# Seven products for eight in every pair's second matrix, and blocks 0 and 1 led through the first matrix together

## The chip, the core and the metric

One core of a Trainium2 chip runs the whole program. The metric is device time of one execution in microseconds (us). The engines of the core are TensorE (PE in the rows: matrix products), VectorE (DVE), ScalarE (ACT), GpSimd (POOL, all but unused here) and SyncE (SP, which issues every transfer). PEld is TensorE's loading of weights, which overlaps the products.

## What is computed

```python
# q, k, v: (8, 8, 576, 64)
k_s = softmax(k, axis=2);  q_s = softmax(q, axis=-1)
kv  = einsum('bhsd,bhse->bhde', k_s, v)
x   = einsum('bhsd,bhde->bhse', q_s, kv)          # 4608 rows of 512
h   = x @ w_in                                    # 512 x 2048
x2  = relu(h)**2 @ w_out                          # 2048 x 512
y   = sigmoid(x2 @ w_gate) * (x2 @ w_val)         # 512 x 1536 each
out = y @ w_out2                                  # 1536 x 512
```

The weights arrive as 64-bit floats, so each 128x512 tile of them is first rebuilt as a 32-bit float by ScalarE and VectorE.

## The kernel before

**Tiles.** The 4608 rows are nine blocks of 512. Every 32-bit factor is split into a high part (a copy to the matrix type, by ScalarE) and a low part (the difference, by VectorE, line 214). `mm3` (lines 217 to 219) makes one product from three matmuls: high·high, high·low, low·high. One matmul has 128x128 weights against 128x512 columns.

**Stages.** Blocks 0, 1 and 2 go through both matrices with plain products while the weights are still being rebuilt: `c_in` multiplies by the first matrix into banks 4 and 5, `c_g` (ScalarE) squares the relu out of the bank into a tile `g0`, `c_hi` and `c_lo` split it, `c_out` multiplies by the second matrix into banks 0 to 3. For each block that is 16 slices f of 12 matmuls in and 12 out. Blocks 3 to 8 go in three pairs (`in_stage`), and then all nine blocks go in five gate stages (`gate_stage`: sigmoid, product, last matrix).

**Seven products.** Where two blocks are taken together, a two-by-two block product is made of seven products of sums instead of eight products (`PRODUCTS`, `plan_seven`). The sums of weights are made once (`plan_sums`). The sums of the data (`plan_b`, `b_comb`, line 671) are VectorE's, and so are the additions of each product out of its bank (`e_add`, line 733). All first matrices of pairs and gates are made so, and the last matrices. The second matrix of a pair is made so only if the pair's number is in `OUT7`, which holds 2, the last pair; pairs 0 and 1 use eight products (`o_mm`).

**Order.** A planner (`Plan`) writes the order of each engine's instructions before the program runs. Each step has a due time (T0, T2, T3 and so on with a step per slice), an engine with a cost, the steps that it waits for, and the buffers that it takes and gives back (`SIZES`: 14 of X, 11 of W, 6 of S, 19 of f, 8 of x). The planner takes the earliest due step that is ready, so a step without urgency fills a gap. Each engine then runs its own list strictly in order, and SyncE its list of transfers.

**Beside the stages** run the k and q steps of later blocks (softmax, small matmuls at lines 440, 452, 467, 524, 577; `plan_blocks`), and the rebuilding, summing, splitting and storing of the gate weights (`plan_w`, spread from T4 until the first gate stage). Split weights are stored to DRAM and fetched again as tiles `ws` for each use. Block 0 uses the tiles `whl` as they are made; block 1 fetches all 16 pieces of the first matrix again. The stages' order is pair 0, pair 1, gate 0, gate 1, pair 2, gates 2 to 4, and the k and q steps for pair 2 stand beside gate 1.

Of the kernel before, what the change touches and what calls it, by code (L numbers as in the profile page):

```python
# [15 lines left out]
AF = mybir.ActivationFunctionType  # L16
# [126 lines left out]
def attention_mlp_mlp(  # L143
# [20 lines left out]
    nc = tc.nc  # L164
    NB, NP, _, N = q.shape
# [5 lines left out]
    KT = DM // 128  # L171
    F1 = w_out.shape[0]
    F2 = w_out2.shape[0]
    wide = w_in.dtype == I64

    OUT7 = (2,)
    SIZES = {"X": 14, "W": 11, "S": 6, "f": 19, "x": 8, "q": 3, "a": 6, "w": 5, "k": 2, "v": 2, "km": 1, "kr": 2, "pa": 2, "qm": 4, "qr": 4}
    cst = ctx.enter_context(tc.tile_pool(name="cst", bufs=1))
    p4 = ctx.enter_context(tc.tile_pool(name="p4", bufs=1))
# [19 lines left out]
    LOW = {DVE: TT}  # L199
# [25 lines left out]
    wf = {}  # L225
# [172 lines left out]

    fetched, xorder, sorder = [], [], []

    def plan_fetch(key, use, t):

        add(t, {DMA: 1.5}, ("wf", use), w_fetch, key, use, after=[("ws",) + key], take=["W"])
        fetched.append(("wf", use))


# [84 lines left out]
    NONE = 3  # L491
# [104 lines left out]
    x_before = {}  # L596
# [105 lines left out]
    freed = {x: [] for x in pairs}  # L702
# [95 lines left out]
    g0 = {}  # L798
    x2d = {}
    z_t = {}  # L800

    def c_use(j, kind, g, i):

        return ("c%d" % j, kind, g, i) if j else (kind, g, i)

    def c_in(j, f, kt):

        g, r = divmod(f // 2, 2)
        w = whl[c_use(j, "in", g, (1, 2, 0, 4)[2 * r + kt // 2])]
        c = 256 * (kt % 2) + 128 * (f % 2)  # L810
        x = x_t[j, kt]
        mm3(banks[4 + f % 2], w[:, 0, c:c + 128], w[:, 1, c:c + 128], x[:, 0], x[:, 1], kt == 0, kt == KT - 1)

    def c_g(j, f):
        t = tile2("f", "g0")
        nc.scalar.activation(out=t, in_=banks[4 + f % 2], func=AF.Relu)
        nc.scalar.activation(out=t, in_=t, func=AF.Square)
        g0[j, f] = t

# [94 lines left out]
    MM = 0.227  # L914
    MH = 0.1185
    NU = F1 // 4
    T0, TS0, TS1 = 30.0, 4.45, 6.2
    TS2 = 3.4
    T2 = T0 + TS0 * F1
    T3 = T2 + TS1 * F1  # L920
    T4 = T3 + TS1 * F1
    T1 = T4 + TS2 * F1 + 4
# [12 lines left out]

    def conv_fetch(j, kind, g, ii, t):

        if j:
            for i in ii:
                plan_fetch((kind, g, i), c_use(j, kind, g, i), t - 14)  # L940

    def conv_in(j, f, t):

        ready = lambda i: ("wf", ("c%d" % j, "in", g, i)) if j else ("wo", "in", g, i)
        tag = "W" if j else "X"
        g, r = divmod(f // 2, 2)
        if f % 2 == 0:
            conv_fetch(j, "in", g, ((1, 2), (0, 4))[r], t)
        for kt in range(KT):
            i = (1, 2, 0, 4)[2 * r + kt // 2]  # L950
            if kt:
                wait = [("ch", j, f, kt - 1)]
            elif f > 1:
                wait = [("cg", j, f - 2)]
            else:
                wait = [("cg", j - 1, F1 - 2 + f)] if j else []
            add(
                t, {PE: 3 * MM}, ("ch", j, f, kt), c_in, j, f, kt,
                after=[("x", j, kt), ready(i)] + wait, give=[XTAG[j]] if f == F1 - 1 else [],
            )  # L960
            if f % 2 and kt % 2:
                add(t, {FREE: 0.0}, ("cf", j, f, kt), lambda: None, after=[("ch", j, f, kt)] + ([] if j else [("ws", "in", g, i)]), give=[tag])
        add(t + 2.6, {ACT: 1.17}, ("cg", j, f), c_g, j, f, after=[("ch", j, f, KT - 1)], take=["f"])

    def conv_out(j, f, t):

        ready = lambda i: ("wf", ("c%d" % j, "out", g, i)) if j else ("wo", "out", g, i)
        tag = "W" if j else "X"
        g, r = divmod(f // 2, 2)
        ii = ((1, 0), (2, 4))[r]  # L970
        if f % 2 == 0:
            conv_fetch(j, "out", g, ii, t)
        add(t - 2.5, {ACT: AS}, ("chi", j, f), c_hi, j, f, after=[("cg", j, f)], take=["S"])
        add(t - 2, LOW, ("clo", j, f), c_lo, j, f, CHOSEN, after=[("chi", j, f)], give=["f"])
# [23 lines left out]
    freed[4, 5] = (T4, [("cg", j, F1 - 2), ("cg", j, F1 - 1)])  # L998

    done_b = {0}  # L1000

    def plan_blocks(js, t, per):

        for j in js:
            new = [b for _, b in segs(j) if b not in done_b]
            done_b.update(new)
            for p in range(NP):
                for b in new:
                    plan_k(b, p, t, 1.0, x_before.get(j, []))
                plan_q(j, p, t + 2, 1.0)  # L1010
                t += per / NP
# [50 lines left out]
    IN = [tuple(range(j, j + 2)) for j in range(NONE, NB, 2)]  # L1062
# [221 lines left out]
    plan_blocks([1], T0 + 6, TS0 * F1 - 20)  # L1284
    plan_blocks([2], T2 + 6, TS1 * F1 - 30)
    plan_blocks(IN[0], T3 + 5, (T1 - T3 - 40) / 2)

    BESIDE = {0: 1, 3: 2}
    t = T1
    for i, (stage, n) in enumerate(STAGES):  # L1290
        if i in BESIDE:
# [6 lines left out]
        t = stage(n, t)  # L1298
# [71 lines left out]
```

## Time and profile before

| | |
|---|---|
| median of 3 runs | 1684.14 us (1682.77 to 1688.67) |
| the profiled execution's own time | 1689.22 us |
| its span, first to last instruction | 1687.4 us |
| mean granted TensorE clock | 0.992 of full |

The page gives an engine's busy time and its count of instructions over the span. Its slices of 42 us show where the load lies. Busy TensorE time is modelled and overlaps from one matmul to the next, so rates are read from the distance between starts.

### The profile page before, as it was taken

Reading aid. Unit: us, or ns where it says so; the run is one execution under the profiler, and the core shown is the slowest. Engines: PE = TensorE matmul, PEld = TensorE weight load, DVE = VectorE, ACT = ScalarE, POOL = GpSimd, SP = SyncE. Lnnn points to the kernel's source line nnn. Section 1 sums busy time; section 2 is a strip of 40 time slices with the busy share of each in tenths; the row PEclk is TensorE's granted clock in tenths of the full one; section 3 lists DMA queues with packets and bytes.
Section 4 is the critical chain, followed back from the end, with each engine's and each line's share of the span. In section 5 each row is a group of like instructions: output and inputs, shape, how many; then the busy total and the mean of one; then the engine's idle time right before and its main releaser. Section 6 shows DMA issues by size and latency. Waiting matters only on the chain.

```text
span 1687.4 us, 24273 instructions
## 1 busy us (share of the span) xinstructions
PE 1651.6 (98%) x8740; PEld 1416.2 (84%) x8740; DVE 1158.9 (69%) x2178; ACT 927.6 (55%) x1632; POOL 1.9 (0%) x14
## 2 busy tenths in 40 slices
PE   6899999999999999999999999999999999999999
PEld 4677788878888888888898889988888899889998
DVE  8988846788889656865774758665954583448446
ACT  5876645567477657643454556464733453335344
POOL 0000000000000000000000000000000000000000
PEclk9998999999999999999999999999999999999999
DMA  7998899798897979899567555867786667555796
GB/s 287 343 359 327 305 360 334 278 342 343 298 347 256 369 256 351 303 335 355 188 191 243 191 186 164 274 201 250 243 291 195 191 210 240 191 196 185 246 377 253
DMA packets 153175, 457.90 MB, mean 271 GB/s; under 512 B 16096, under 2 KB 25312, under 8 KB 153056
## 3 DMA queue, kind: packets, MB, share of 16 engines
q1 hardware_dynamic: 153056, 456.36, 77.4%
q8 instruction: 69, 1.13, 0.3%
q14 instruction: 50, 0.41, 0.1%
HBM read 360.35 MB, written 95.94 MB: 270 GB/s over the span
## 4 chain that ended last, share of the span: by engine, by line
PE 90%; DVE 5%; DMA 2%; ACT 2%; issue 1%; SPq 0%; ACTq 0%; DVEq 0%
PE bank L217 29%; PE bank L219 28%; PE bank L218 28%; PE kps L467 2%; PE xps L577 2%; DMA ws<-w_in 1%; DVE bX L214 0%; DMA wraw<-in_moe_w_out_dram 0%; DVE whl L214 0%; DVE bS L214 0%; DMA kt<-in_k_dram 0%; DVE xf L671 0%; PE qsw L524 0%; DVE wf L277 0%; DVE s L671 0%
## 5 line engine op out<-in xcount | busy, mean ns | idle before, releaser
L217 PE MATMUL bank<-bX,ws 128*128 128x512 f32 (+1 forms) x1176 | 447.2, 380 | 3.2 <-DMA ws<-w_in 3.2
L218 PE MATMUL bank<-bX,ws 128*128 128x512 f32 (+1 forms) x1176 | 441.3, 375 | 0.0
L219 PE MATMUL bank<-bX,ws 128*128 128x512 f32 (+1 forms) x1176 | 441.2, 375 | 0.0
L733 DVE TENSOR_TENSOR s<-s,bank 128x512 f32<-128x512 f32 (+1 forms) x285 | 184.4, 652 | 206.6 <-PE bank L219 170.6
L211 ACT ACTIVATE s<-bank 128x512 f32<-128x512 f32 (+1 forms) x285 | 161.4, 570 | 225.9 <-PE bank L219 223.5
L217 PEld LDWEIGHTS bank<-bX,ws 128*128 128x128 f32 x1176 | 222.4, 189 | 42.3 <-ACT bS L211 3.5
L219 PEld LDWEIGHTS bank<-bX,ws 128*128 128x128 f32 x1176 | 222.1, 189 | 40.4
L218 PEld LDWEIGHTS bank<-bX,ws 128*128 128x128 f32 x1176 | 222.5, 189 | 37.9 <-issue 0.7
L211 ACT ACTIVATE bS<-s 128x512 fp32r<-128x512 f32 (+1 forms) x298 | 174.9, 598 | 124.4 <-PE bank L219 113.0
L214 DVE TENSOR_TENSOR bS<-s,bS 128x512 fp32r<-128x512 f32 (+1 forms) x298 | 191.6, 652 | 57.5 <-ACT bS L211 57.0
L217 PE MATMUL bank<-ws,bS 128*128 128x256 f32 x756 | 214.7, 284 | 0.0
L219 PE MATMUL bank<-ws,bS 128*128 128x256 f32 x756 | 214.1, 283 | 0.4 <-DVE bS L214 0.4
L218 PE MATMUL bank<-ws,bS 128*128 128x256 f32 x756 | 214.0, 283 | 0.0
L752 ACT ACTIVATE s<-s 128x512 f32<-128x512 f32 (+1 forms) x120 | 70.5, 589 | 140.2 <-DVE s L733 139.9
L217 PEld LDWEIGHTS bank<-ws,bS 128*128 128x128 f32 x756 | 145.0, 192 | 1.4 <-ACT s L211 0.3
L218 PEld LDWEIGHTS bank<-ws,bS 128*128 128x128 f32 x756 | 145.0, 192 | 1.0 <-issue 0.2
L219 PEld LDWEIGHTS bank<-ws,bS 128*128 128x128 f32 x756 | 145.0, 192 | 0.6 <-DVE bS L214 0.6
L217 PE MATMUL bank<-bS,ws 128*128 128x512 f32 x368 | 144.6, 393 | 0.2 <-issue 0.2
L218 PE MATMUL bank<-bS,ws 128*128 128x512 f32 x368 | 143.3, 389 | 0.0
L219 PE MATMUL bank<-bS,ws 128*128 128x512 f32 x368 | 143.3, 389 | 0.0
L211 ACT ACTIVATE whl<-wf 128x512 fp32r<-128x512 f32 x127 | 78.3, 626 | 50.1 <-DVE wf L284 27.8
L214 DVE TENSOR_TENSOR whl<-wf,whl 128x512 fp32r<-128x512 f32 x127 | 85.9, 689 | 10.1 <-ACT whl L211 9.9
(118 smaller groups left out, 2425.3 us busy)
## 6 DMA issues: line engine op xcount, KB each, us to landing
ws<-w_gv SPq DMA_DIRECT2D x210, 512.0 KB, 4.4
ws<-w_out SPq DMA_DIRECT2D x197, 512.0 KB, 4.3
ws<-w_in SPq DMA_DIRECT2D x116, 512.0 KB, 6.1
w_out<-whl SPq DMA_DIRECT2D x53, 512.0 KB, 4.7
w_gv<-whl SPq DMA_DIRECT2D x42, 512.0 KB, 6.2
w_in<-whl SPq DMA_DIRECT2D x32, 512.0 KB, 4.9
wraw<-in_moe_w_out_dram SPq DMA_DIRECT2D x28, 512.0 KB, 6.6
vt<-in_v_dram SPq DMA_DIRECT2D x32, 325.0 KB, 6.5
```

The source lines that it names most:

```text
L211: nc.scalar.activation(out=dst, in_=src, func=AF.Copy)
L214: by_name[engine].tensor_tensor(out=dst, in0=src, in1=hi.bitcast(F32), op=ALU.subtract)
L217: nc.tensor.matmul(ps, ah, bh, start=first, stop=False, skip_group_check=True)
L218: nc.tensor.matmul(ps, ah, bl, start=False, stop=False, skip_group_check=True)
L219: nc.tensor.matmul(ps, al, bh, start=False, stop=last, skip_group_check=True)
L467: nc.tensor.matmul(ps[:, 0:2 * D + 1], kt[:, r, :], vt[:, r, 0:2 * D + 1], start=(r == 0), stop=(r == RK - 1))
L577: nc.tensor.matmul(ps[:, e], kvf[b % 2][p], t[:, e], start=True, stop=True)
L733: nc.vector.tensor_tensor(out=t, in0=t, in1=banks[pr[b]][:, 0:n], op=ALU.add)
L752: nc.scalar.activation(out=t, in_=t, func=AF.Sigmoid)
```

## The change

Three things are edited. `OUT7` becomes all three pairs, so the second matrix of pairs 0 and 1 takes seven products too. Blocks 0 and 1 share the first matrix: a sequence `SEQ` takes four slices of block 0 (`LEAD`), then alternates block 1's slice f with block 0's slice f+4, then block 2; both blocks read the same `whl` tiles, block 1 fetches none, and eight of block 1's `g0` tiles lie in x buffers (`KEPT`). The second matrix of blocks 0, 1 and 2 follows, and due times are reset for that. The stages' order becomes pairs 0, 1, 2 and then gates 0 to 4, with the k and q steps of pair 2 beside pair 1.

```diff
-    OUT7 = (2,)
+    OUT7 = (0,1,2)
+    LEAD = 4
...
+    KEPT = 8
+    SEQ = [(0, f) for f in range(LEAD)]
+    for f in range(F1):
+        SEQ += [(1, f)] + ([(0, f + LEAD)] if f + LEAD < F1 else [])
+    SEQ += [(2, f) for f in range(F1)]
+    PLACE = {x: n for n, x in enumerate(SEQ)}
+
+    def fetched_(j, kind):
+        return j > 1 if kind == "in" else j > 0
+
+    def gtag(j, f):
+        return "x" if j == 1 and f < KEPT else "f"
+
+    def c_bank(j, f):
+        return 4 + PLACE[j, f] % 2
...
-        return ("c%d" % j, kind, g, i) if j else (kind, g, i)
+        return ("c%d" % j, kind, g, i) if fetched_(j, kind) else (kind, g, i)
...
-    T0, TS0, TS1 = 30.0, 4.45, 6.2
+    T0, TS0 = 28.0, 4.6
...
-            elif f > 1:
-                wait = [("cg", j, f - 2)]
             else:
-                wait = [("cg", j - 1, F1 - 2 + f)] if j else []
+                wait = [("cg",) + SEQ[place - 2]] if place > 1 else []
...
-    for f in range(F1):
-        conv_in(0, f, T0 + TS0 * f)
-    for j, T in ((1, T2), (2, T3)):
-        for f in range(F1):
-            conv_in(j, f, T + TS1 * f)
-            conv_out(j - 1, f, T + TS1 * f + 3)
...
+    items = [(TI[j][f], conv_in, j, f) for j, f in SEQ] + [(TC[j][f], conv_out, j, f) for j in range(NONE) for f in range(F1)]
+    for t, fn, j, f in sorted(items, key=lambda x: x[0]):
+        fn(j, f, t)
+    plan.chain([("chi", j, f) for j in range(NONE) for f in range(F1)])
...
-    STAGES = [(in_stage, 0), (in_stage, 1), (gate_stage, 0), (gate_stage, 1), (in_stage, 2), (gate_stage, 2), (gate_stage, 3), (gate_stage, 4)]
+    STAGES = [(in_stage, n) for n in range(len(IN))] + [(gate_stage, n) for n in range(len(GATE))]
...
-    BESIDE = {0: 1, 3: 2}
+    BESIDE = {0: 1, 1: 2}
```

In the order of instructions below, a row names the line, the operation, and the tile written from the tiles read, with their numbers. TensorE in the first matrix, before: block 0 alone, here the end of a slice in bank 5, on the tile whl_882.

```order
L217 MATMUL bank5_93<-x0_309,whl_882 128x512
L218 MATMUL bank5_93<-x0_309,whl_882 128x512
L219 MATMUL bank5_93<-x0_309,whl_882 128x512
L217 MATMUL bank5_93<-x0_352,whl_882 128x512
L218 MATMUL bank5_93<-x0_352,whl_882 128x512
L219 MATMUL bank5_93<-x0_352,whl_882 128x512
```

TensorE at the joint stage now (x0_641 and x0_735 are block 1's data, x0_309 and x0_353 block 0's):

```order
L218 MATMUL bank4_92<-x0_641,whl_832 128x512
L219 MATMUL bank4_92<-x0_641,whl_832 128x512
L220 MATMUL bank4_92<-x0_641,whl_832 128x512
L218 MATMUL bank5_93<-x0_353,whl_1090 128x512
L219 MATMUL bank5_93<-x0_353,whl_1090 128x512
L220 MATMUL bank5_93<-x0_353,whl_1090 128x512
L218 MATMUL bank4_92<-x0_735,whl_832 128x512
```

Block 1's slices from a tile that block 0 used before stand between block 0's slices from a newer tile; no fetched tile `ws` occurs.

VectorE, where block 2 ends and pair 0 begins, before: low parts of block 2's last slices (g0hl) among the rebuilding of a weight tile (wf).

```order
L214 TENSOR_TENSOR g0hl_3321<-g0_2945,g0hl_3321 128x512
L284 ISA wf_3327<-wraw_3276,wf_3327 128x1024
L214 TENSOR_TENSOR bX_3349<-xf_2360,bX_3349 128x512
L214 TENSOR_TENSOR bX_3353<-xf_2553,bX_3353 128x512
L671 TENSOR_TENSOR xf_2823<-xf_3144,xf_2823 128x512
```

The same place now, VectorE's instructions 576 to 582:

```order
L215 TENSOR_TENSOR g0hl_3227<-g0_2542,g0hl_3227 128x512
L215 TENSOR_TENSOR whl_3229<-wf_3051,whl_3229 128x512
L215 TENSOR_TENSOR g0hl_3240<-g0_2594,g0hl_3240 128x512
L215 TENSOR_TENSOR whl_3242<-wf_3056,whl_3242 128x512
L215 TENSOR_TENSOR bX_3262<-xf_2414,bX_3262 128x512
L215 TENSOR_TENSOR bX_3264<-xf_2133,bX_3264 128x512
L672 TENSOR_TENSOR xf_2414<-xf_3025,xf_2414 128x512
```

Instruction 578 (g0hl_3240) waits for ScalarE, and through it for TensorE's instruction 1297, which gives back an S buffer.

VectorE in the second matrix of pair 0, before: no sums of data, only low parts (bS).

```order
L214 TENSOR_TENSOR bS_3633<-s1_3551,bS_3633 128x512
L430 TENSOR_TENSOR kmx_3645<-kt_3622 128x256
L434 TENSOR_TENSOR kmx_3645<-kmx_3645,kt_3622 128x128
L733 TENSOR_TENSOR s5_3573<-s5_3573,bank4_92 128x512
L434 TENSOR_TENSOR kmx_3645<-kmx_3645 128x128
```

The same place now:

```order
L215 TENSOR_TENSOR bS_3756<-s1_3297,bS_3756 128x512
L672 TENSOR_TENSOR s1_3297<-s2_3577,s1_3297 128x512
L672 TENSOR_TENSOR s2_3577<-s5_3492,s2_3577 128x512
L215 TENSOR_TENSOR bS_3771<-s1_3356,bS_3771 128x512
```

A sum (line 672) stands behind each low part that it follows, on the engine that also runs the k and q steps.

## Rows read from the trace of the kernel before

**Rows 1.** The page: busy time of each engine, then slices.

```profile
PE 1651.6 (98%) x8740; PEld 1416.2 (84%) x8740; DVE 1158.9 (69%) x2178; ACT 927.6 (55%) x1632; POOL 1.9 (0%) x14
...
DVE  8988846788889656865774758665954583448446
...
PEclk9998999999999999999999999999999999999999
```

**Rows 2.** Windows, all instructions: stretch, its length, each engine's busy time.

```profile
core 0: us, PE busy (x) PEld busy (x) DVE busy (x) ACT busy (x) POOL busy (x), PEclk, DMA share, GB/s
31.50:72.00 40.50, 37.91 (x178) 28.96 (x178) 39.22 (x91) 33.57 (x62) 0.00 (x0) 0.96 0.98 343
72.00:200.00 128.00, 119.07 (x532) 96.27 (x531) 116.23 (x249) 89.38 (x162) 0.00 (x0) 0.93 0.94 339
200.00:361.00 161.00, 160.77 (x765) 133.82 (x763) 110.57 (x226) 87.76 (x154) 0.00 (x0) 1.00 0.86 318
361.00:386.50 25.50, 21.38 (x80) 16.91 (x81) 15.91 (x29) 12.44 (x22) 0.00 (x0) 0.87 1.01 382
386.50:722.00 335.50, 335.50 (x1548) 278.94 (x1547) 258.73 (x490) 219.98 (x391) 0.00 (x0) 1.00 0.88 314
```

**Rows 3.** Windows of line 217 alone, the first of each three matmuls.

```profile
31.50:72.00 40.50, 18.07 (x40) 7.95 (x40) 0.96 0.98 343
72.00:200.00 128.00, 57.65 (x134) 26.54 (x135) 0.93 0.94 339
200.00:361.00 161.00, 84.33 (x205) 38.41 (x204) 1.00 0.86 318
361.00:386.50 25.50, 12.06 (x27) 5.75 (x27) 0.87 1.01 382
```

**Rows 4.** Windows of line 440 alone, one matmul for each k tile.

```profile
31.50:72.00 40.50, 0.87 (x3) 0.42 (x3) 0.96 0.98 343
72.00:200.00 128.00, 1.63 (x6) 0.84 (x6) 0.93 0.94 339
200.00:361.00 161.00, 1.91 (x7) 0.98 (x7) 1.00 0.86 318
```

**Rows 5.** TensorE's timeline: start, length, instruction; 25 matmuls from first to last.

```profile
600.12 0.39 PE L219 MATMUL bank<-bS,ws 128*128 128x512 f32 x1
...
605.78 0.39 PE L217 MATMUL bank<-bS,ws 128*128 128x512 f32 x1
```

**Rows 6.** TensorE's timeline, idle time and its releaser in brackets.

```profile
192.48 0.80 PE L467 MATMUL kps<-vt,kt 128*128 128x129 f32 x2 [2.73 <-ACT kt L461]
```

**Rows 7.** Windows of half clock, all instructions.

```profile
191.70:198.70 7.00, 6.22 (x20) 5.35 (x21) 5.80 (x16) 4.45 (x10) 0.00 (x0) 0.51 0.96 377
379.50:386.40 6.90, 5.75 (x14) 4.57 (x15) 3.29 (x8) 1.96 (x4) 0.00 (x0) 0.51 1.03 408
```

**Rows 8.** TensorE's waits from 340 to 420 us: total, times, longest.

```profile
PE bank L217 <- DMA ws<-w_in: 3.2, 1, 3.2
PE bank L217 <- DMA ws<-w_out: 1.2, 1, 1.2
```

**Rows 9.** VectorE's timeline where it runs without a gap.

```profile
1040.14 0.68 DVE L214 TENSOR_TENSOR bS<-s,bS 128x512 fp32r<-128x512 f32 x1
1040.74 0.69 DVE L671 TENSOR_TENSOR s<-s,s 128x512 f32<-128x512 f32 x1
```

**Rows 10.** Windows of pair 0's halves, pair 1, and a dense stretch, all instructions.

```profile
357.00:454.00 97.00, 92.65 (x429) 76.36 (x428) 78.37 (x163) 62.44 (x112) 0.00 (x0) 0.96 0.91 336
454.00:545.00 91.00, 91.00 (x435) 75.71 (x434) 81.49 (x165) 65.36 (x119) 0.00 (x0) 1.00 0.86 297
545.00:640.00 95.00, 95.00 (x420) 78.65 (x420) 56.83 (x95) 52.24 (x88) 0.00 (x0) 1.00 0.88 314
640.00:722.00 82.00, 82.00 (x363) 67.92 (x362) 61.96 (x106) 54.46 (x97) 0.00 (x0) 1.00 0.90 324
1036.00:1080.00 44.00, 43.64 (x353) 42.70 (x353) 43.00 (x74) 28.60 (x50) 0.00 (x0) 1.00 0.69 225
```

More of the change, by code (lines that the diff above doesn't have):

```diff
@@ L399, in attention_mlp_mlp, with plan_fetch @@
     fetched, xorder, sorder = [], [], []
-    def plan_fetch(key, use, t):
-        add(t, {DMA: 1.5}, ("wf", use), w_fetch, key, use, after=[("ws",) + key], take=["W"])
+    def plan_fetch(key, use, t, wait=()):
+        add(t, {DMA: 1.5}, ("wf", use), w_fetch, key, use, after=[("ws",) + key, *wait], take=["W"])
         fetched.append(("wf", use))
@@ L800, in attention_mlp_mlp @@
     z_t = {}
+    JOINT = (0, 1)
+    KEPT = 8
[10 more added lines that the diff above has]
+        return 4 + PLACE[j, f] % 2
     def c_use(j, kind, g, i):
-        return ("c%d" % j, kind, g, i) if j else (kind, g, i)
+        return ("c%d" % j, kind, g, i) if fetched_(j, kind) else (kind, g, i)
     def c_in(j, f, kt):
@@ L811, in c_in @@
         x = x_t[j, kt]
-        mm3(banks[4 + f % 2], w[:, 0, c:c + 128], w[:, 1, c:c + 128], x[:, 0], x[:, 1], kt == 0, kt == KT - 1)
+        mm3(banks[c_bank(j, f)], w[:, 0, c:c + 128], w[:, 1, c:c + 128], x[:, 0], x[:, 1], kt == 0, kt == KT - 1)
     def c_g(j, f):
-        t = tile2("f", "g0")
-        nc.scalar.activation(out=t, in_=banks[4 + f % 2], func=AF.Relu)
+        t = tile2(gtag(j, f), "g0")
+        nc.scalar.activation(out=t, in_=banks[c_bank(j, f)], func=AF.Relu)
         nc.scalar.activation(out=t, in_=t, func=AF.Square)
@@ L916, in attention_mlp_mlp @@
     NU = F1 // 4
-    T0, TS0, TS1 = 30.0, 4.45, 6.2
[L918 to L922, printed above, removed]
+    T0, TS0 = 28.0, 4.6
+    TJ = [T0 + TS0 * f for f in range(F1)]
+    T2 = TJ[-1] + 4
+    TI = [TJ, [TJ[min(f + LEAD, F1 - 1)] + (2 if f + LEAD < F1 else 2.8 * (f + LEAD - F1 + 1)) for f in range(F1)]]
+    TC = [[T2 + 5.6 * f for f in range(F1)]]
+    TI.append([T2 + 2.8 * LEAD + 5.0 * f for f in range(F1)])
+    T3 = TC[0][-1] + 4
+    TC.append([T3 + 3.6 * f for f in range(F1)])
+    T4 = TC[1][-1] + 3.6
+    TC.append([T4 + 3.4 * f for f in range(F1)])
+    T1 = TC[2][-1] + 7
     for p in range(NP):
@@ L927, in attention_mlp_mlp @@
     for g in range(NU):
-        plan_first("in", g, [T0 + TS0 * (4 * g + 2 * (b // 2)) for b in range(4)], "w")
+        plan_first("in", g, [TI[0][4 * g + 2 * (b // 2)] for b in range(4)], "w")
     for g in range(NU):
-        plan_first("out", g, [T2 + TS1 * (4 * g + 2 * (b % 2)) + 3 for b in range(4)], "w")
+        plan_first("out", g, [TC[0][4 * g + 2 * (b % 2)] for b in range(4)], "w")
     for g in range(NU):
@@ L936, in conv_fetch @@
     def conv_fetch(j, kind, g, ii, t):
-        if j:
+        if fetched_(j, kind):
             for i in ii:
-                plan_fetch((kind, g, i), c_use(j, kind, g, i), t - 14)
+                plan_fetch((kind, g, i), c_use(j, kind, g, i), t - 14, [("qa", j, NP - 1)] if kind == "in" else [])
     def conv_in(j, f, t):
-        ready = lambda i: ("wf", ("c%d" % j, "in", g, i)) if j else ("wo", "in", g, i)
-        tag = "W" if j else "X"
+        ready = lambda i: ("wf", ("c%d" % j, "in", g, i)) if fetched_(j, "in") else ("wo", "in", g, i)
         g, r = divmod(f // 2, 2)
@@ L948, in conv_in @@
             conv_fetch(j, "in", g, ((1, 2), (0, 4))[r], t)
+        place = PLACE[j, f]
         for kt in range(KT):
@@ L960, in conv_in @@
             )
-            if f % 2 and kt % 2:
-                add(t, {FREE: 0.0}, ("cf", j, f, kt), lambda: None, after=[("ch", j, f, kt)] + ([] if j else [("ws", "in", g, i)]), give=[tag])
-        add(t + 2.6, {ACT: 1.17}, ("cg", j, f), c_g, j, f, after=[("ch", j, f, KT - 1)], take=["f"])
+            if f % 2 and kt % 2 and j:
+                add(
+                    t, {FREE: 0.0}, ("cf", j, f, kt), lambda: None,
+                    after=[("ch", j, f, kt)] + ([] if j > 1 else [("ch", 0, f, kt), ("ws", "in", g, i)]), give=["W" if j > 1 else "X"],
+                )
+        add(t + 2.6, {ACT: 1.17}, ("cg", j, f), c_g, j, f, after=[("ch", j, f, KT - 1)], take=[gtag(j, f)])
     def conv_out(j, f, t):
@@ L973, in conv_out @@
         add(t - 2.5, {ACT: AS}, ("chi", j, f), c_hi, j, f, after=[("cg", j, f)], take=["S"])
-        add(t - 2, LOW, ("clo", j, f), c_lo, j, f, CHOSEN, after=[("chi", j, f)], give=["f"])
+        add(t - 2, LOW, ("clo", j, f), c_lo, j, f, CHOSEN, after=[("chi", j, f)], give=[gtag(j, f)])
         if f:
@@ L985, in conv_out @@
                 add(t + 4, {DMA: 0.8}, ("ost", j, o, 1), c_st, j, o, after=[("cev", j, o)], give=["a"])
-    for f in range(F1):
-        conv_in(0, f, T0 + TS0 * f)
-    for j, T in ((1, T2), (2, T3)):
-        for f in range(F1):
-            conv_in(j, f, T + TS1 * f)
-            conv_out(j - 1, f, T + TS1 * f + 3)
-    for f in range(F1):
-        conv_out(NONE - 1, f, T4 + TS2 * f)
+    items = [(TI[j][f], conv_in, j, f) for j, f in SEQ] + [(TC[j][f], conv_out, j, f) for j in range(NONE) for f in range(F1)]
+    for t, fn, j, f in sorted(items, key=lambda x: x[0]):
+        fn(j, f, t)
+    plan.chain([("chi", j, f) for j in range(NONE) for f in range(F1)])
     j = NONE - 1
@@ L997, in attention_mlp_mlp @@
     freed[2, 3] = (T1 + 2, [("cev", j, 2), ("cev", j, 3)])
-    freed[4, 5] = (T4, [("cg", j, F1 - 2), ("cg", j, F1 - 1)])
+    freed[4, 5] = (T4, [("cg",) + x for x in SEQ[-2:]])
     done_b = {0}
@@ L1273, in gate_stage @@
         return t
-    STAGES = [(in_stage, 0), (in_stage, 1), (gate_stage, 0), (gate_stage, 1), (in_stage, 2), (gate_stage, 2), (gate_stage, 3), (gate_stage, 4)]
-    before = []
+    STAGES = [(in_stage, n) for n in range(len(IN))] + [(gate_stage, n) for n in range(len(GATE))]
+    before = [("qa", NONE - 1, NP - 1)]
     for stage, n in STAGES:
@@ L1283, in attention_mlp_mlp @@
             before = [("xl", "x2", j, kt) for j in GATE[n] for kt in range(KT)]
-    plan_blocks([1], T0 + 6, TS0 * F1 - 20)
-    plan_blocks([2], T2 + 6, TS1 * F1 - 30)
+    x_before[2] = [("wg", "in", NU - 1, 0)]
+    plan_blocks([1], T0 - 4, 24)
+    plan_blocks([2], TI[2][0] - 40, 30)
     plan_blocks(IN[0], T3 + 5, (T1 - T3 - 40) / 2)
-    BESIDE = {0: 1, 3: 2}
+    BESIDE = {0: 1, 1: 2}
     t = T1
```

## The prediction

> **What bounds the kernel now.** The page first: TensorE is busy for 98 per cent of the span and VectorE for 69, but the slices show VectorE at 8 and 9 tenths for the first five, and TensorE's granted clock below full there and once more near 380 us [rows 1]. So one engine bounds most of the run and two compete at its start; the windows say by how much. At full clock 25 matmuls of 512 columns take 605.78 − 600.12 = 5.66 us, 0.2264 each [rows 5]. Line 217 opens each group of three, so its count times three is the work done.
>
> From 200 to 361 us TensorE hardly waits and the clock is full [rows 2]: 3 × 205 × 0.2264 = 139.2 us of products [rows 3], and the other 21.8 us belong to the k and q matmuls of 7 k tiles [rows 4], 3.1 us for each. With these two prices the lost time elsewhere follows. 31.5 to 72: 3 × 40 × 0.2264 + 3 × 3.1 = 36.5 of 40.5 us, 4 lost. 72 to 200: 3 × 134 × 0.2264 + 6 × 3.1 = 109.6 of 128 us, 18.4 lost. There VectorE is busy 116.2 of 128 us [rows 2], and TensorE's order makes it wait for k tiles in the making (2.73 us at 192.48, released by ScalarE's exponential of a k tile) [rows 6]; behind that wait the clock is granted at 0.51, the level of 1.2 GHz, for 7 us [rows 7]. 361 to 386.5: 3 × 27 × 0.2264 = 18.3 of 25.5 us, 7.2 lost, of which 4.4 are two waits for fetched weights [rows 8] and about 3.4 the half clock from 379.5 to 386.4 [rows 7]. After that TensorE is full to the end of pair 1 [rows 2].
>
> **The change, part by part.** All sums are against the profiled execution, 1689.2 us (span 1687.4); it lies 5.1 us over the median, and I carry the difference to the median 1684.1.
>
> *Matmuls.* A half of a pair's second matrix has 8 × 24 matmuls before and 7 × 24 now. Two halves in two pairs make 96 fewer, which the order of instructions confirms (8428 to 8332). 96 × 0.2264 = −21.7 us, if TensorE is fed.
>
> *The start.* Until 72 us the order is nearly the same and VectorE sets the pace, so the 4 us there stay. Then each rebuilt tile of the first matrix feeds two blocks. Blocks 0 and 1 in the first matrix are 384 matmuls, 87 us, from tiles that VectorE finished by about 90 us before. TensorE starts at 31.5 us, so it is busy with these until at least 118 us, and with the k and q steps until about 130. In that time VectorE gets ahead with the second matrix's tiles, for which TensorE waited before. So of the 18.4 us I expect some 3 to remain, for k tiles that are still late: −15.5. The bounds are −18.4 and 0, the latter if the k and q steps of block 1, now due earlier, displace the rebuilding one for one.
>
> *Fetches.* Block 1's 16 fetches of 512 KB go, and 4 × 6 come, because seven products want 14 fetches in a half where eight wanted 8. SyncE's list grows from 1006 to 1014. The cost of these is a rival below. The 7.2 us lost at 361 to 386.5 belong to a jam of that list (DMA share 1.01 [rows 2]); I take them out here, because pair 0 gets its whole new price in the next part.
>
> *VectorE in the pairs.* Its list grows by 131 instructions, nearly all of them 512-column operations (48 more low parts, 64 sums, 18 more additions). Run without a gap, one costs 0.60 us from start to start [rows 9], so 79 us in two pairs. Before, it was busy 78.4 + 81.5 us in pair 0 (188 us) and 56.8 + 62.0 in pair 1 (177 us) [rows 10], and the k and q steps of pair 2 now also fall beside pair 1. That can't all hide. The order of instructions gives the tightest stretch. VectorE's instruction 578 waits, through ScalarE, for TensorE's 1297. TensorE's 2908, the first product of pair 2, waits for VectorE's 1307. Between them VectorE has 730 instructions: 518 at 0.60 us, 16 transposes and 12 of 640 columns somewhat longer, 60 of half the length and 124 small ones, 366 us without any gap. TensorE has 1465 matmuls and the k and q steps of 12 k tiles, 332 + 38 = 370 us. So the two are level over 370 us, and every gap on VectorE beyond four us is a gap on TensorE. Right behind instruction 578 VectorE is even behind: its 93 instructions up to number 670 make 46.8 us, against 39 us on TensorE, so 8 us are lost even without a gap. How dense VectorE can run has two ends: 43.0 of 44 us (0.977) in the stretch from 1036, and 81.5 of 91 (0.896) in the second half of pair 0 [rows 10]. At 0.977 the 366 us become 375 and the loss is 8, set by the first piece; at 0.896 they become 408 and the loss is 38. I take 0.95, between the two and near the 0.968 of 31.5 to 72 [rows 2]: 385 − 370 = +15 us. VectorE's queue is in order, so behind a late low part or sum stand the additions that free banks; TensorE waits for those.
>
> *The clock.* Waits of a few us were followed by half clock before [rows 6, 7]. Spread over many small waits I expect one more stretch of 7 us, which costs 3.5: +4, bounds 0 and 10.
>
> *The rest.* ScalarE gets 52 more copies and loses 16 of 18 table loads; it is busy 55 per cent [rows 1] and beside the path. The order of the gate stages costs nothing: their work is the same, and the gate weights get more time, since the first gate comes a pair later.
>
> Sum: −21.7 − 15.5 − 7.2 + 15 + 4 = −25.4. Profiled 1664, on the median 1684.1 − 25.4 = 1659 us. The likeliest case has a range of its own, 1648 to 1670.
>
> **The rivals.**
>
> *VectorE stays hidden* (gain in full). Before, VectorE was busy 81.5 of 91 us without a gap on TensorE [rows 10], which speaks for it; the level count of 366 against 370 us speaks against it. The pairs would lose nothing: −21.7 − 15.5 − 7.2 = −44.4, 1640 us. The Trainium skill (Perfetto Trace Analysis, Identifying the Most-Contended Engine) says to optimize the engine of highest occupancy first, which over the whole run is TensorE, and the engine with 69 per cent would then not count. By that rule 1640 is the forecast; the trace agrees for the whole and disagrees for the pairs, where occupancy must be taken by stage.
>
> *VectorE takes the gain back.* It runs at 0.896 as in the second half of pair 0: +38 for +15, so −2.4 and 1682 us, no change that can be told.
>
> *The start does not gain.* The joint stage waits for the same tiles as before: the 15.5 us are lost, 1675 us, still faster.
>
> *Transfers decide, and it is slower.* From block 2's second matrix to the first gate stage (TensorE's instructions 1250 to 3750, 572 us of work) SyncE's list holds 198.7 MB, 347 GB/s. The windows moved 314 GB/s at a share of 0.88, 339 at 0.94 and 382 at 1.01 [rows 2], so it fits by little. If the list delivers only the 314 GB/s of the pairs before, because a store that waits for VectorE holds the fetches behind it, the stretch takes 633 us, 61 more than its work: −44.4 + 61 = +17, 1701 us. It decides against the change when the rate falls under 198.7 MB / 616 us = 323 GB/s. For it speaks that TensorE's only long waits after 200 us were for fetches [rows 8]; against it, that the average before was what the work asked for, not a limit.
>
> **How the numbers follow.** Likeliest case 0.45, VectorE hidden 0.17, start without gain 0.11, gain taken back 0.15, transfers 0.12. A measurement can tell 0.3 per cent, 5 us. Faster: 0.45 + 0.17 + 0.11 + 0.02 of the fourth case = 0.75; same: 0.13; slower: 0.12. The range 1640 to 1686 takes in the hidden case and the case of the gain taken back, and leaves out the transfers and a little below 1640.
>
> **What would show it.** Right: matmuls of line 218 (217 before) spaced 0.226 us through 130 to 300 us, block 2's second matrix ending near 350 us where it ended at 366, VectorE over 9 tenths from there to the end of pair 2, and TensorE's waits in that stretch released by VectorE (low parts bS and additions), 10 to 25 us in all. Wrong: waits released by DMA in the pairs over 10 us, half clock for more than 20 us after 330, or block 2 ending later than 360.

## The result, and the profile after

| | before | after |
|---|---|---|
| median | 1683.66 us (1682.77 to 1688.67, 4 runs) | 1665.55 us (1664.55 to 1667.48, 4 runs) |
| profiled execution | 1689.22 us, span 1687.4 | 1664.55 us, span 1662.8 |

The ratio is 0.9884 [0.9865, 0.9903]: 18 us less, against 25 forecast. The changed kernel's page, busy time of each engine and the slices of 42 us that answer to [rows 1]:

```profile
PE 1625.5 (98%) x8644; PEld 1392.9 (84%) x8644; DVE 1227.3 (74%) x2309; ACT 937.1 (56%) x1668; POOL 2.0 (0%) x14
...
DVE  8986785889999999999796486347724684448446
...
PEclk9999999999999999999999999999999999999999
```

VectorE is now full from the tenth slice to the nineteenth, 374 to 790 us, where before it had 5 to 8 tenths from the fourteenth slice to the nineteenth [rows 1]. TensorE, at 98 per cent, seems not to mind. The windows (columns as in [rows 2]) show where it does:

```profile
31.50:72.00 40.50, 36.49 (x178) 27.12 (x177) 39.03 (x94) 30.70 (x57) 0.00 (x0) 0.97 0.75 270
72.00:200.00 128.00, 126.67 (x598) 104.57 (x597) 98.21 (x206) 90.09 (x159) 0.00 (x0) 1.00 0.77 277
200.00:340.00 140.00, 137.46 (x659) 113.41 (x658) 106.97 (x223) 76.99 (x136) 0.00 (x0) 1.00 0.94 347
340.00:400.00 60.00, 51.46 (x223) 42.07 (x222) 55.44 (x114) 38.24 (x68) 0.00 (x0) 0.91 0.89 321
400.00:880.00 480.00, 478.54 (x2182) 393.09 (x2181) 455.33 (x853) 347.55 (x618) 0.00 (x0) 1.00 0.91 330
```

The last two stretches in the kernel before, from its own windows:

```profile
340.00:400.00 60.00, 55.65 (x238) 45.04 (x237) 47.77 (x89) 38.53 (x68) 0.00 (x0) 0.94 0.97 367
400.00:880.00 480.00, 480.00 (x2352) 406.00 (x2351) 356.06 (x643) 285.53 (x500) 0.00 (x0) 1.00 0.83 296
```

From 72 to 200 us, TensorE now runs 598 matmuls where it ran 532 [rows 2], with no half clock. From 340 to 400 us it has 223 where it had 238. From 400 to 880 VectorE does 99 us more and TensorE hardly waits. TensorE's waits from 340 to 400 us (total, times, longest):

```profile
PE bank L218 <- DVE s L734: 4.2, 1, 4.2
PE kps L468 <- ACT kt L462: 2.2, 1, 2.2
PE bank L218 <- DMA ws<-w_in: 1.0, 1, 1.0
PE qsw L525 <- DVE qst L533: 0.9, 1, 0.9
```

Two stretches of half clock, one among these waits and one that begins half a microsecond after the longest ends (windows, all instructions):

```profile
364.90:371.70 6.80, 5.84 (x16) 4.48 (x16) 6.12 (x15) 2.90 (x7) 0.00 (x0) 0.50 0.99 361
385.40:388.80 3.40, 3.40 (x9) 2.65 (x8) 3.33 (x9) 3.31 (x7) 0.00 (x0) 0.50 1.02 375
```

And what stands ahead of the bank addition for which TensorE waits 4.15 us, in the timeline:

```profile
379.57 0.71 DVE L559 STREAM_TRANSPOSE qtr<-qt 128x512 f32<-128x512 f32 x1
380.20 0.39 DVE L271 TENSOR_SCALAR wf<-wf 128x512 int32<-128x512 int32 x1
380.51 0.68 DVE L215 TENSOR_TENSOR whl<-wf,whl 128x512 fp32r<-128x512 f32 x1
381.11 0.69 DVE L278 SCALAR_TENSOR_TENSOR wf<-wraw,wf 128x512 int32<-128x512 int32 x1
381.71 0.68 DVE L734 TENSOR_TENSOR s<-s,bank 128x512 f32<-128x512 f32 x1
382.30 0.69 DVE L285 CUSTOM_DVE_ANT_0 wf<-wraw,wf 128x1024 uint16<-128x1024 uint16 x1
382.90 0.68 DVE L734 TENSOR_TENSOR s<-s,bank 128x512 f32<-128x512 f32 x1
383.50 0.69 DVE L215 TENSOR_TENSOR whl<-wf,whl 128x512 fp32r<-128x512 f32 x1
384.11 2.48 DVE L734 TENSOR_TENSOR s<-s,bank 128x512 f32<-128x512 f32 x4
384.85 0.50 PE L218 MATMUL bank<-bX,ws 128*128 128x512 f32 x1 [4.15 <-DVE s L734]
```

VectorE never stops here. Between the additions stand rebuilding steps and low parts of weights (lines 271, 278, 285, and 215 into whl), among them those of the gate weights, which nothing needs until gate 0, some 470 us later. The gate weights are not the only ones. The summed weights of the first matrix, which the pairs do need, are late too. SyncE's stores of both kinds (the tile w_in from 225 to 420 us, w_gv from 300 to 450; the row gives shortest, median and longest duration in ns, then the first and last start), before (line 302) and after (line 303):

```profile
L302 SPq DMA_DIRECT2D w_in<-whl x16: 319/323/1433, 234.8 to 347.6; - x16
L302 SPq DMA_DIRECT2D w_gv<-whl x15: 319/327/856, 348.3 to 426.7; - x15
L303 SPq DMA_DIRECT2D w_in<-whl x16: 319/320/452, 258.8 to 387.1; - x16
L303 SPq DMA_DIRECT2D w_gv<-whl x12: 319/320/424, 351.8 to 444.0; - x12
```

Before, the last store of the first matrix is issued at 347.6 us, ahead of the end of block 2's second matrix at 366. Now it is issued at 387.1, and block 2 ends at 356.

**A measure for the rest.** For each moment I take the time passed, less what the matmuls that TensorE had started by then cost at their usual distance: 0.2267 us for 512 columns, 0.120 for 256, in the k and q steps 0.43 for 512 columns and in proportion below that, 0.11 for 128 and 0.07 for 16. That is TensorE's lost time so far, waits and half clock together. It is worked out from the starts in the one trace of each kernel:

| kernel | lost by 350 us | 350 to 400 | 400 to 1500 | median us |
|---|---|---|---|---|
| before | 50.9 | 8.2 | 6.4 | 1683.66 |
| after | 39.7 | 14.7 | 8.1 | 1665.55 |
| e_seven | 45.9 | 7.2 | 55.2 | 1710.35 |
| e_orderonly | 48.8 | 4.3 | 5.9 | 1681.46 |
| e_split | 47.7 | 4.7 | 12.4 | 1668.66 |
| e_joint | 41.2 | 12.8 | 5.5 | 1683.35 |
| e_order | 41.8 | 23.5 | 48.1 | 1712.40 |
| e_nosums | 42.2 | 15.1 | 7.3 | 1665.01 |
| e_late20 | 40.3 | 0.9 | 30.7 | 1674.24 |
| e_late80 | 40.0 | 1.0 | 46.0 | 1692.47 |
| e_spread58 | 39.2 | 0.9 | 21.6 | 1662.91 |
| e_spread65 | 40.3 | 0.9 | 9.6 | 1653.85 |
| e_spread70 | 40.2 | 0.9 | 8.6 | 1653.05 |
| e_split_spread | 45.4 | 0.9 | 9.9 | 1658.34 |

Work at the usual distance is 1617.5 us with eight products in pairs 0 and 1 and 1595.7 with seven: −21.8, the forecast's first term.

### The profile page after: what moved, and what is told of

It reads as the page before. It is cut to its first block, busy times and chain, and to the rows that moved or that the text cites. A ratio compares the mean times of both kernels' runs of the same rounds, so it can differ in the third digit from the quotient of the medians.

```text
span 1662.8 us, 24384 instructions
## 1 busy us (share of the span) xinstructions
PE 1625.5 (98%) x8644; PEld 1392.9 (84%) x8644; DVE 1227.3 (74%) x2309; ACT 937.1 (56%) x1668; POOL 2.0 (0%) x14
## 4 chain that ended last, share of the span: by engine, by line
PE 85%; DVE 7%; DMA 4%; ACT 2%; issue 1%; SPq 1%; DVEq 0%; ACTq 0%
PE bank L218 27%; PE bank L220 27%; PE bank L219 27%; DMA wraw<-in_moe_w_out_dram 2%; PE xps L578 1%; PE kps L468 1%; DVE whl L215 1%; DVE wf L299 1%; DMA wraw<-in_moe_w_in_dram 1%; DVE wf L285 1%; DVE wf L278 1%; DMA qt<-in_q_dram 1%; DVE bX L215 0%; DMA ws<-w_in 0%; PE qsw L525 0%
## 5 line engine op out<-in xcount | busy, mean ns | idle before, releaser
L734 DVE TENSOR_TENSOR s<-s,bank 128x512 f32<-128x512 f32 (+1 forms) x297 | 191.9, 654 | 213.9 <-PE bank L220 175.6
L212 ACT ACTIVATE s<-bank 128x512 f32<-128x512 f32 (+1 forms) x297 | 168.4, 572 | 217.6 <-PE bank L220 213.9
L212 ACT ACTIVATE bS<-s 128x512 fp32r<-128x512 f32 (+1 forms) x330 | 194.6, 601 | 131.9 <-PE bank L220 119.4
L215 DVE TENSOR_TENSOR bS<-s,bS 128x512 fp32r<-128x512 f32 (+1 forms) x330 | 214.2, 656 | 60.2 <-ACT bS L212 59.8
L218 PE MATMUL bank<-bS,ws 128*128 128x512 f32 x336 | 133.5, 397 | 1.2 <-ACT bX L212 1.1
L219 PE MATMUL bank<-bS,ws 128*128 128x512 f32 x336 | 131.2, 391 | 0.0
L220 PE MATMUL bank<-bS,ws 128*128 128x512 f32 x336 | 131.0, 390 | 0.0
L672 DVE TENSOR_TENSOR s<-s,s 128x512 f32<-128x512 f32 (+1 forms) x192 | 122.2, 655 | 1.7 <-ACT s L740 0.2
L212 ACT ACTIVATE whl<-wf 128x512 fp32r<-128x512 f32 x127 | 79.3, 628 | 39.2 <-DVE wf L285 16.1
```

Of the source, the lines that this page charges most:

```text
L212: nc.scalar.activation(out=dst, in_=src, func=AF.Copy)
L215: by_name[engine].tensor_tensor(out=dst, in0=src, in1=hi.bitcast(F32), op=ALU.subtract)
L672: by_name[engine].tensor_tensor(out=t[o], in0=t[a], in1=t[b], op=ALU.subtract)
L734: nc.vector.tensor_tensor(out=t, in0=t, in1=banks[pr[b]][:, 0:n], op=ALU.add)
```

## The experiments

The medians of the kernel before, on the chips of these runs, lay between 1682.84 and 1684.76 us.

### The parts alone

**Seven products alone** (e_seven: the kernel before with one line changed).

```diff
-    OUT7 = (2,)
+    OUT7 = (0,1,2)
```

> The kernel before with one edit: seven products in all three pairs (the start and the stages' order as before). Theory P (the price is paid at pair 0's beginning, where VectorE's list holds gate weights and sums ahead of the bank additions): 96 matmuls less, -21.7 us, and 12 to 15 us back between 360 and 420 us, so 1672 to 1676, with VectorE's slice after 420 us not costing more than 5. Rival V (VectorE is too full over the whole of both pairs, since here the gate weights must be done before gate 0 that follows pair 1): the loss goes on from 420 to 650 us, 1678 to 1686. Rival H (the sums are hidden): 1660 to 1664.

Measured: 1710.35 us, ratio 1.0159 [1.0133, 1.0186], 27 us slower, worse than any theory; rival V's reason, gate weights that must be done before a gate 0 behind pair 1, comes nearest. Nothing extra is lost at 360 to 400 us; 55 us are lost after it. Its window 540 to 780 us, then TensorE's waits from 400 to 880 us:

```profile
540.00:780.00 240.00, 215.66 (x895) 174.75 (x896) 200.22 (x341) 147.65 (x258) 0.00 (x0) 0.93 0.92 337
```

```profile
PE bank L217 <- DMA ws<-w_out: 19.0, 4, 9.7
PE bank L217 <- ACT wraw L260: 8.0, 1, 8.0
PE bank L217 <- DMA ws<-w_in: 3.2, 1, 3.2
```

TensorE waits for fetched tiles, and once until ScalarE has finished with a raw gate weight (wraw), a tile of the same 11 W buffers. The DMA share is 0.92, hardly above the 0.86 to 0.91 at which the same pairs were fed before [rows 10]. So the DMA engines had hardly more to do than when they kept up, which points to the planned list: with gate 0 behind pair 1, all the gate weights must be prepared within two pairs, in the buffers and on the VectorE that seven products need more of.

**The joint start and the new order of stages, without the seven products** (e_joint: the changed kernel with one line changed back).

```diff
-    OUT7 = (0,1,2)
+    OUT7 = (2,)
```

> The changed kernel with eight products again in the second matrices of pairs 0 and 1, so that the joint start and the new order of stages stand alone. Theory P: the start is worth 11 us against the profiled execution of before and 5 to 11 against its median, the order some 3, so 1670 to 1676; and at pair 0's beginning (360 to 400 us) TensorE loses under 8 us where the changed kernel loses 14, as the sums of the second matrix are gone there. Rival S (the start's gain is only the before's disturbed clock in its one profiled execution): 1680 to 1684. Rival T (the loss at 360 to 400 comes from the start's transfers and has nothing to do with the seven products): the same 14 us are lost there.

Measured: 1683.35 us, ratio 1.0004 [0.9991, 1.0017]. The time is rival S's, but not by its reason: by 350 us the start has gained 4.2 to 9.7 us over the five kernels that start as before (41.2 us lost against 45.4 to 50.9). Then 12.8 us are lost by 400, where the four of those that leave the gate weights in their place lose 4.3 to 8.2. Rival T is right that the same waits come without the seven products; that the start's transfers cause them, as it holds, the runs on the gate weights below do not bear out. The window and the waits from 340 to 400 us:

```profile
340.00:400.00 60.00, 53.64 (x231) 43.70 (x230) 55.08 (x111) 41.91 (x77) 0.00 (x0) 0.91 0.88 319
```

```profile
PE bank L218 <- DVE s L734: 2.6, 1, 2.6
PE kps L468 <- ACT kt L462: 2.2, 1, 2.2
```

**The old order of stages under the rest of the change** (e_order).

```diff
-    STAGES = [(in_stage, n) for n in range(len(IN))] + [(gate_stage, n) for n in range(len(GATE))]
+    STAGES = [(in_stage, 0), (in_stage, 1), (gate_stage, 0), (gate_stage, 1), (in_stage, 2), (gate_stage, 2), (gate_stage, 3), (gate_stage, 4)]
-    BESIDE = {0: 1, 1: 2}
+    BESIDE = {0: 1, 3: 2}
```

> The changed kernel with the stages in the order of before (pair 0, pair 1, gate 0, gate 1, pair 2, gates 2 to 4; the k and q steps of pair 2 beside gate 1). Theory P: the order gives the 2.9 us that TensorE lost after 850 us in before and no longer loses, by k and q steps beside a gate whose ScalarE swaps its tables; here they come back, and the gate weights have to be done one pair earlier on a VectorE that is full: 1668 to 1674. Rival O (the order makes no difference by itself): 1664 to 1667.

Measured: 1712.40 us, ratio 1.0177 [1.0152, 1.0202]. Both theories fall. Beside 0.9884 for the changed kernel, the order is worth 2.9 per cent, some 49 us, which is far more than the products save. From 370 to 780 us TensorE waits most for what it waited for in e_seven, raw gate weights and fetched tiles:

```profile
PE bank L218 <- ACT wraw L261: 16.8, 2, 9.8
PE bank L218 <- DMA ws<-w_out: 6.4, 1, 6.4
```

**Seven products with the new order and the old start (e_split); the new order alone (e_orderonly).** In the kernel before, the two edits above the other way round, with and without `OUT7 = (0,1,2)`.

> The kernel before with seven products in every pair and the new order of stages (pairs 0, 1, 2, then the gates; pair 2's k and q steps beside pair 1), but the start as before: blocks 0 and 1 one after the other. Theory Q (the earlier runs: the two edits only work together, the joint start gives back at 360 to 400 us what it gains by 350): 21.7 us less of matmuls and 2 to 5 back, 1661 to 1668, no different from the changed kernel. Rival J (the joint start is worth its 10 us, and the loss at 360 to 400 is the seven products' own): 1673 to 1680. Rival E (seven products need the joint start's free tiles and transfers): over 1685, as with seven products alone.

> The kernel before with the new order of stages alone (eight products in the second matrices of pairs 0 and 1, start as before). Theory Q: the order by itself only takes away the 2 to 4 us that TensorE loses after 850 us, 1679 to 1684. Rival O2 (the room that it gives the gate weights is worth something without seven products too): under 1678. Rival O3 (the moved k and q steps cost what they save): 1684 to 1688.

Measured: 1668.66 us, ratio 0.9912 [0.9897, 0.9927], and 1681.46 us, 0.9987 [0.9975, 1.0]. The new order is worth little alone, and the seven products lose 27 us alone; together they are worth 15. That is nearly all of the change. The joint start adds 0.28 per cent, 5 us, with overlapping intervals. Theory Q comes nearest, though 1668.66 lies just above its range; its "no difference" is not refuted by these intervals.

### What is late at 360 to 400 us

**VectorE lighter, the lists in the same order** (e_nosums). For the second matrices of pairs 0 and 1 the 64 sums are left out, so their products are of unsummed tiles.

```diff
+        if nm[0] == "G" and nm[1] < 2:
+            return
         by_name[engine].tensor_tensor(out=t[o], in0=t[a], in1=t[b], op=ALU.subtract)
```

> The changed kernel without VectorE's sums of the data for the second matrices of pairs 0 and 1 (64 subtractions left out, some 38 us of VectorE; the products are then of the unsummed tiles), all else and the lists of all engines in the same order. Theory P: these sums stand mostly behind the crowded stretch, and what is late at 360 to 400 us are bank additions behind gate weights; 2 to 6 us less than the changed kernel, 1659 to 1664. Rival V (VectorE's fullness over the whole of the pairs sets the time): 8 us or more less, under 1657. Rival H (VectorE costs nothing): no difference, 1664 to 1667.

Measured: 1665.01 us, ratio 0.9898 [0.9877, 0.9919]: no difference, rival H. Its window:

```profile
400.00:880.00 480.00, 479.03 (x2191) 394.35 (x2190) 424.21 (x795) 344.56 (x617) 0.00 (x0) 1.00 0.91 331
```

VectorE is 31 us less busy than in the changed kernel over these 480 us, and TensorE gains half a microsecond of busy time. So VectorE's 455 of 480 us there did not set the time.

**The gate weights later** (e_late20, e_late80). They were spread from T4, the due start of block 2's second matrix, in nine groups (`plan_w`); now from 20 or 80 us after T1, pair 0's due start, up to the same end. These are due times: in the traces the first raw gate weight is fetched at 365 and 421 us instead of 338, so 27 and 83 us later, and not the 60 and 120 of the expectations.

```diff
-                plan_w(kind, g, T4 + (t + 40 - T4) / len(preps) * m, 10.0, "w")
+                plan_w(kind, g, T1 + 20 + (t + 40 - T1 - 20) / len(preps) * m, 10.0, "w")
```

> The changed kernel with the gate weights' preparation spread from 20 us after pair 0's due start instead of from the start of block 2's second matrix (some 60 us later). Theory W (what makes VectorE late at 340 to 400 us is the some 25 us of gate weights in its list there): the 4.2 us wait for a bank addition, the k-tile wait of 2.2 and the half-clock stretches behind them shrink, TensorE loses 3 to 8 us less there: 1656 to 1662. Rival K (the k and q steps and the sums of pair 0 make it late by themselves): no difference, 1664 to 1667. Rival C (the preparation, now crowded into less time, collides later, as in the run with seven products alone): 1668 or more, with the loss after 540 us.

> As the run with the gate weights 60 us later, now 120 us later. Theory W: as that one at 340 to 400 us, and with two pairs and a half left for them not yet crowded: 1655 to 1664. Rival K: 1664 to 1667. Rival C: 1675 or more, with waits for transfers and weight tiles in pairs 1 and 2.

Measured: 1674.24 us, ratio 0.995 [0.9933, 0.9966], and 1692.47, 1.0053 [1.0037, 1.0068]. In the place in question theory W is more right than it claimed: the loss of 14.7 us becomes 0.9, and TensorE has no wait left. The last store of the first matrix's summed weights comes at 360 to 361 us in both runs (387 in the changed kernel). With the gate weights, their copies on ScalarE, their transfers and their buffers moved as well, and the planner wrote all lists anew; the runs show that their place decides, and not which of these it is. For VectorE speak the rows above, where the additions stand behind them. The first run's windows, and the 30 us in which it loses most:

```profile
340.00:400.00 60.00, 60.00 (x284) 49.88 (x284) 53.16 (x106) 42.77 (x77) 0.00 (x0) 1.00 0.93 337
400.00:540.00 140.00, 134.29 (x633) 109.61 (x632) 135.41 (x269) 97.61 (x175) 0.00 (x0) 1.00 0.85 308
500.00:530.00 30.00, 25.79 (x109) 19.73 (x107) 30.00 (x52) 17.27 (x31) 0.00 (x0) 1.00 0.83 291
```

In all, rival C: in e_late20 what is gained there is lost again at 500 to 540, 700 to 740 and 860 to 900 us, about 8 us each. These are the beginnings of pair 1, pair 2 and gate 0, when the next stage's sums come on top and VectorE runs without a gap (30.00 of 30 us from 500 to 530). In e_late80 the losses are spread from 500 to 900 us, and at 902 us TensorE waits 7.4 us for a fetched gate weight: there the weights are too late themselves. In e_late20, from 500 to 545 us:

```profile
PE bank L219 <- DVE bS L215: 3.4, 4, 1.8
PE bank L218 <- ACT bS L212: 2.2, 1, 2.2
```

### A version that beats both

Both runs suggest that VectorE has a backlog, and that its height at a stage's beginning is what matters. So the first six groups get a wide step (65 us in e_spread65, 58 in e_spread58), and the three groups of the last matrix, needed only some 115 us into gate 0, go to pair 2's end and into gate 0, where VectorE was busy 14 of 30 us at 890 to 920.

```diff
-                plan_w(kind, g, T4 + (t + 40 - T4) / len(preps) * m, 10.0, "w")
+                plan_w(kind, g, ([T1 + 20 + 65 * x for x in range(6)] + [735, 810, 855])[m], 10.0, "w")
```

> The changed kernel with the gate weights' preparation (nine groups, some 14 us of VectorE each) begun as in the run that began it 60 us later, but with 65 us from group to group as in the changed kernel, and the three groups of the last matrix moved to the end of pair 2 and into gate 0, where VectorE is half idle. Theory B (a backlog: VectorE is full from 340 to 880 us, and TensorE waits wherever a stage's first sums stand behind it): the 13 us kept at 360 to 400 stay kept, and with two groups (28 us) gone from before 880 us the three losses of 8 us at 500, 700 and 870 us shrink to 2 to 4 each: 1653 to 1661. Rival M (moved work only moves the wait): the losses stay or pass into gate 0, 1664 to 1676.

> As the run with 65 us from group to group, with 58 for the first six. Theory B: a little more of VectorE's work before 700 us, so the losses at 500 and 700 us are 1 to 3 us larger than with 65: 1654 to 1664. Rival M: 1664 to 1676.

Measured: 1653.85 us, ratio 0.9823 [0.9809, 0.9837], and 1662.91 us, 0.9876 [0.9862, 0.989]. Theory B. Windows with 65:

```profile
340.00:400.00 60.00, 60.00 (x284) 49.90 (x283) 53.20 (x106) 42.73 (x77) 0.00 (x0) 1.00 0.94 334
400.00:880.00 480.00, 478.65 (x2181) 393.23 (x2181) 446.24 (x832) 333.19 (x592) 0.00 (x0) 1.00 0.89 319
```

Nine us less of VectorE from 400 to 880 than in the changed kernel, and the 14 us at 360 to 400 are kept. With 58 it is 9 us slower, not the 1 to 3 expected: lost time rises by 6 us from 500 to 540 and again from 700 to 740 us, where with 65 it rises by 1.2 and 0.1. The runs also part the two edits. In e_spread58 the first raw weights of the first six groups are fetched within 15 us of where e_late20 fetches them, and the three last groups come 50 to 82 us later: mostly this took 1674.24 to 1662.91, and the wider step the other 9 us.

**The same with the old start (e_split_spread), and with a step of 70 (e_spread70)** (`T1 + 20 + 70 * x`; last groups at T1 + 430, 505 and 550 in both).

> The start as before, seven products in every pair, the new order, and the gate weights spread as in the run with 65 us from group to group (their times counted from pair 0's due start in both). Theory G (the joint start is worth its 9 us as soon as the backlog at 360 to 400 us no longer takes them): the lag of TensorE when pair 0 begins is 49 us here and 40 there, so 9 us more than that run: 1660 to 1666. Rival Z (the spreading only repairs what the joint start causes and does nothing here): 1667 to 1670. Rival J3 (the joint start is worth 3 us, as between the changed kernel and the run without it): 1655 to 1658.

> As the run with 65 us from group to group, with 70 for the first six groups. Theory B: some of the 6 us that TensorE still loses from 500 to 720 us go, 1650 to 1654. Rival M2 (the fifth and sixth group now run into pair 2's end and gate 0's first sums): a wait of 3 us with a half-clock stretch behind it, 1657 to 1664.

Measured: 1658.34 us, ratio 0.9849 [0.983, 0.9869], and 1653.05 us, 0.9812 [0.9799, 0.9826], the best. Against e_spread65 the joint start is now worth 4 to 5 us, between theory G's 9 and rival J3's 3; the intervals of the ratios overlap, but the traces say the same, 45.4 us lost by 350 here (and not the 49 expected) and 40.3 there. The page of the best, busy time and VectorE's slices:

```profile
PE 1620.9 (98%) x8644; PEld 1389.8 (84%) x8644; DVE 1229.7 (75%) x2307; ACT 938.6 (57%) x1674; POOL 1.9 (0%) x14
...
DVE  8986785889999999988797795447724783458446
```

VectorE does the same work as in the changed kernel (1229.7 against 1227.3 us); only its place differs, and with it the planned lists of the other engines.

## Why the prediction came out, step by step

The sum was −25.4 against the profiled execution, and between the two profiled executions it is −24.8 by the table (−21.8 of work, and 65.5 − 62.5 = 3.0 less lost) and −24.7 by their times. The first term held. That the sum fits to 0.6 us is luck: the start gave 4.3 us less than forecast, and the stretch behind it took 3.6 us less. Between the medians the change is −18.1, and 1665.55 lies 6.5 us above the 1659 forecast, inside the likeliest case's 1648 to 1670.

- *Matmuls*, −21.7: right, −21.8.
- *Start*, −15.5, bounds −18.4 and 0: it measured −11.2 by 350 us. The mechanism is right: the spacing is that of a fed TensorE,

```profile
199.68 0.39 PE L218 MATMUL bank<-g0hl,whl 128*128 128x512 f32 x1
...
205.80 0.39 PE L218 MATMUL bank<-g0hl,whl 128*128 128x512 f32 x1
```

  28 starts, (205.80 − 199.68) / 27 = 0.2267 us, and block 2's second matrix ends at 356 us instead of 366 (350 was forecast). But the execution it was counted against lost 50.9 us by 350, and the four other kernels that start as before lost 45.4 to 48.8: their half clock at 160 to 200 us was shorter or absent. Before's profiled execution lay 5.6 us above its median and after's 1.0 below, which is the gap between −24.7 in the profiles and −18.1 in the medians; the long half clock at the start may well make most of the 5.6, but no execution at the median was profiled. A start compared with such an execution should have been priced lower.
- *Waits for transfers*, −7.2, *VectorE in the pairs*, +15, and *the clock*, +4: they belong together, since the old waits were taken out to give pair 0 its whole new price. Together they are +11.8; after 350 us the loss grew from 14.6 to 22.8, by 8.2. (One reading in it was off: in [rows 6, 7] the half clock begins at 191.7 us, within the wait that ends at 192.48 and not behind it.) The place was right. VectorE's instructions 578 and 1307, and the first product of pair 2 behind the latter (the row at 721.77 merges 1307 with the next):

```profile
334.53 0.69 DVE L215 TENSOR_TENSOR g0hl<-g,g0hl 128x512 fp32r<-128x512 f32 x1 [1.42 <-ACT g0hl L212]
721.77 1.32 DVE L734 TENSOR_TENSOR xp<-xp,bank 128x512 f32<-128x512 f32 x2
722.54 0.50 PE L218 MATMUL bank<-bX,ws 128*128 128x512 f32 x1
```

  The stretch took 388 us where 385 were forecast, and TensorE lost some 21 us in it by the measure above, for 15 and 4. The first piece, up to instruction 670, was to take 46.8 us without a gap and to cost 8. It took 50, and 670 is the addition at 384.11 us that ends TensorE's wait of 4.15; some 13 us were lost by then.
- *What the +15 was charged to* is the part that failed: the 131 instructions that seven products add. e_nosums took 64 of them away, 31 us of VectorE, and gained nothing; e_joint has no seven products in these pairs and loses 12.8 us from 350 to 400 all the same. Full is not late: what costs is what stands ahead of the first additions where a stage begins. The joint start brings pair 0 forward by 10 us while the gate weights stay nearly where they were (first store at 352 us for 348), so the two collide; with the gate weights later, the loss from 350 to 400 falls from 14.7 to 0.9.
- *A jam of transfers at 361 to 386 us* was to be eased. Its waits for fetched weights did shrink, from 4.4 to 1.0 us, but the loss from 350 to 400 grew from 8.2 to 14.7, and VectorE's additions now lead it.
- *"The order of the gate stages costs nothing"*: true as far as it goes, and the largest omission. I noted that the gate weights get more time, and gave it no price. Without it the same change is 29 us slower than before (e_order). The rival "transfers decide" had its price (+17) and its mechanism, a fetch held up behind other work in the list, nearly as e_seven and e_order then showed it; what decided between them was this step. The rate of 323 GB/s tells nothing apart: from 400 to 880 us those two moved 312 and 316, but the kernel before moved 296 without a wait.

Of the signs, VectorE over 9 tenths held, as did waits for transfers under 10 us and half clock under 20 (10.2). TensorE's waits released by VectorE were fewer than the 10 to 25 us: 5.1 from 340 to 400 us, before none of its products is such a wait named from 400 to 1120. Block 2's second matrix ended between the 350 forecast and the 360 that would have been a sign of being wrong.

The Trainium skill (Perfetto Trace Analysis, Optimization Strategy) says that where the most-contended engine changes between regimes, interleaving the regimes can help. The runs fit that: with VectorE's weight work moved later, out of pair 0's beginning and the last of it into gate 0, the time fell by 12 us (ratio 0.9884 to 0.9812) with no work removed.

What stays open: how much of e_seven's loss is W buffers and how much VectorE, and how much of the loss at 350 to 400 us goes away by a lighter VectorE there and how much by ScalarE and the transfers that moved with it, which no run separated; and why the half clock at 130 to 200 us differs between kernels with the same start.

## What to carry to other kernels

Work that fills gaps has a place all the same: look for what stands ahead of the first bank additions of each stage on an in-order engine, and move work with a far deadline out of there before removing any. Price each part of a joint change in the company of the others, since here two parts, one losing 27 us and the other gaining 1 alone, gained 15 together. And take the start of a kernel from several executions, if one has a longer half clock than its median allows.

## What the runs showed of the hardware

A wait can cost up to double. From 360 to 400 us the changed kernel has 8.3 us of waits in four rows and 10.2 us at half clock, worth 5.1 more, of 14.7 lost by 400. In e_late20 the waits of 2.4 and 3.4 us that end at 709 and 872 us come with 3.4 and 6.8 us of half clock, while five waits of up to 2.2 us between 500 and 545 had none. In e_spread58 waits of 1.5 and 2.2 us that end at 527 and 530 come with 3.4 us of it, so the length of a wait alone does not tell. Nor is the clock what makes the time jump there: of the 12 us that e_spread58 loses more than e_spread65 after 400 us, 1.7 are half clock and the rest waits and other gaps. By contrast a VectorE at 97 per cent of a stretch (234 of 240 us from 540 to 780, after) left TensorE without a named wait of over 1.1 us.
